# A decode step of attention and an MLP: TensorE's program in loops, a fixed home for V, and w4 loaded ahead of K

## The chip, the cores and the metric

The kernel runs on one core of a Trainium2 chip. The metric is the device time of one execution in microseconds (us); lower is better. The engines are called by the profile's names: PE (TensorE), DVE (VectorE), ACT (ScalarE), POOL (GpSimd) and SP (SyncE), which issues the large loads. PSUM is the memory that PE writes to, in eight banks of 128 x 512 float32 each.

## The reference

One token, x of 1024 values, passes a layernorm and then two branches whose results are added:

```
xn  = layernorm(x)
A:  q = xn @ wq                                     # 32 heads of 128
    scores = q . k_cache * 128**-0.5                # 4 key heads, 65536 keys each, 8 query heads share one
    o = softmax(scores) @ v_cache ;  A = o @ wo     # wo is 4096 x 1024
B:  h  = gelu(layernorm(xn) @ w1) ; hs = shift(h) @ w2      # with one position every shifted value is zero
    x1 = xn + hs ; B = x1 + gelu(layernorm(x1) @ w3) @ w4   # w3 1024 x 3584, w4 3584 x 1024
out = x + A + B
```

All inputs are bfloat16. The two caches hold 4 x 65536 x 128 values each, 67 MB apiece; the weights together are about 36 MB. Every byte is used once.

## The kernel before

**Homes.** Three slots of 64 KB per partition lie in the on-chip memory. A cache is cut into eight tiles of 32768 keys: tile 0 and 1 belong to the first key head, 2 and 3 to the second, and so on. A K or a V tile fills a slot, 8.4 MB. Work items go through the three slots in turn:

```
wq, K0, V0, w3, K1, V1, wa, K2, V2, K3, V3, K4, V4, K5, V5, K6, V6, K7, wb, V7, wo
```

Here wa is w1 with the first half of w4, and wb is the second half of w4 with w2. Item i+3 is loaded by SP when item i has been used, so SP's queue normally holds one or two loads that have not begun. Only wo differs: it takes the slot of K7 and is loaded in five pieces of 10, 10, 8, 3 and 1 rows (a row is 1024 columns of one chunk of wo).

**One K tile** (`compute_K`). DVE transposes the tile in four quarters (L449, viewed as float32, so pairs of bfloat16 values move together). PE multiplies: 64 products of 128 x 512 into four banks `sc` (L455), in a loop over the banks, started after two quarters and again after four; in the last tile after every quarter. DVE takes the maximum over `sc` (L462), two tiny PE transposes with three small DVE steps between them make a maximum per query head (L463 to L469), ACT takes the exponential (L471), and DVE transposes the result into `work` (L473).

**One V tile** (`compute_V`). PE forms 64 products from `work` and the V slot into the bank `oacc` (L503), four at a time in four column strips of the array. After the first tile of a head ACT copies `oacc` away (L509). After the second, `group_weights` and `group_end` put the two tiles together: weighted sums on DVE (L488, L491, L515), one PE product (L521), a division and a reduction on DVE (L523 to L529). This fills 32 rows of `oT`, the operand of wo. wo's products need all four heads in `oT`.

**The ends.** wq, w3 and w1 are multiplied with 32 columns at once in strips (`rows_product`, L321). w4, w2 and the first ten rows of wo run in `rows_loop` (L337): a loop on PE, two products of 512 columns for each row, one column of results, two rows to a pass (five for wo). The other 22 rows of wo run unrolled in `compute_wo`, as four products of 256 columns in four strips (L536). A copy on DVE (L560) and one store end the kernel.

**Order.** `Flow` records each operation's reads and writes, and emits a wait on the semaphore of the engine or load that it needs. All engines run the recorded order; nothing moves it afterwards.

Of the kernel before, what the change touches and what calls it, by code (L numbers as in the profile page):

```python
# [6 lines left out]

BF16 = mybir.dt.bfloat16
# [8 lines left out]
WO_PIECES = (10, 10, 8, 3, 1)  # L17
WO_UNROLL = 5
CGS = 2


class Flow:


    def __init__(self, nc, ctx):
        self.nc = nc
        self.ctx = ctx
        self.engines = {"T": nc.tensor, "V": nc.vector, "S": nc.scalar, "G": nc.gpsimd, "Q": nc.sync}
        self.sems = {}
        self.counts = {}  # L30
        self.seen = {e: {} for e in self.engines}
        self.writer = {}
        self.readers = {}

    def sem(self, name):
        if name not in self.sems:
            self.sems[name] = self.ctx.enter_context(self.nc.semaphore(f"s_{name}"))
            self.counts[name] = 0
        return self.sems[name]

    def _wait(self, eng, reads, writes):
# [7 lines left out]
        for key in reads:  # L49
            if key in self.writer:  # L50
                token = self.writer[key]
                if token[0] != "T" or eng != "T":
                    add(token)
        for key in writes:
            if key in self.writer:
                token = self.writer[key]
                if token[0] != "T" or eng != "T":
                    add(token)
            for token in self.readers.get(key, ()):
                if token[0] != eng:  # L60
                    add(token)
        for name, value in need.items():
            if self.seen[eng].get(name, 0) < value:
                self.engines[eng].wait_ge(self.sem(name), value)
                self.seen[eng][name] = value
# [8 lines left out]
    def op(self, eng, reads, writes, emit, times=1):  # L74

        self._wait(eng, reads, writes)
        sem = self.sem(eng)

        def signal(ins):
            ins.then_inc(sem, 1)  # L80

        emit(signal)
        self.counts[eng] += times
        self._note((eng, self.counts[eng]), reads, writes)
# [8 lines left out]
    def one(self, eng, reads, writes, call):  # L93
        self.op(eng, reads, writes, lambda signal: signal(call(self.engines[eng])))
# [3 lines left out]
def kernel(  # L98
# [28 lines left out]
    assert S == 1 and DH == P and REP == 8 and HQ == 32 and DC == 8 and NOUT == 1024  # L127
# [4 lines left out]
    FW = F // 8  # L132
    assert FW <= 512 and F % 8 == 0 and FW % 16 == 0 and FW // 16 == FC and OC == 32
    NQ = NOUT // 4
    NH = NOUT // 2
    FH = FC // 2
# [9 lines left out]
    slots = [tile_sb([P, KEYS], BF16, f"slot{i}") for i in range(SLOTS)]  # L146
    work = tile_sb([P, HF * 512], BF16, "work")
    ob = tile_sb([P, 512], F32, "ob")
    xpad = tile_sb([P, DC, 32], BF16, "xpad")
    QS = P + 24  # L150
    qst = [tile_sb([P, 4, QS], BF16, f"qst{i}") for i in range(2)]
    qsel = tile_sb([P, 4, HQ], BF16, "qsel")
    ident_bf = tile_sb([P, P], BF16, "ident_bf")
    ident_f = tile_sb([P, P], F32, "ident_f")
    og = tile_sb([P, P + 1], F32, "og")
    msk = tile_sb([P, 4, 32], F32, "msk")
    hstrip = tile_sb([P, 192], BF16, "hstrip")
    gsel = tile_sb([P, P], BF16, "gsel")
    sel32 = tile_sb([P, 32], F32, "sel32")
    sel8 = tile_sb([P, 8], F32, "sel8")  # L160
    sel8x = tile_sb([P, 32], F32, "sel8x")
    mask16 = tile_sb([P, 16], F32, "mask16")
    mask64 = tile_sb([P, 64], F32, "mask64")
# [3 lines left out]
    lnb = tile_sb([P, 8, DC], F32, "lnb")  # L167
    x_bf = tile_sb([P, DC], BF16, "x_bf")
    xn2b = tile_sb([P, DC], BF16, "xn2b")
    qT = tile_sb([P, HQ], BF16, "qT")  # L170
    hf_f = tile_sb([P, FC], F32, "hf_f")
    hT = tile_sb([P, FC], BF16, "hT")
    gT = tile_sb([P, DC], BF16, "gT")
    o5 = tile_sb([P, 32], F32, "o5")
    oT = tile_sb([P, OC], BF16, "oT")
    rep = msk[0:1].rearrange("p a b -> p (a b)")

    sc = ps.tile([P, HF, 512], F32, name="sc")
    oacc = ps.tile([P, 512], F32, name="oacc")
    pm = ps.tile([P, 512], F32, name="pm")  # L180
    psR = ps.tile([P, 2, 512], F32, name="psR")
    psB = sc[:, 0, :]
# [7 lines left out]
    assert sum(WO_PIECES) == OC  # L190
    wo_start = [sum(WO_PIECES[:i]) for i in range(len(WO_PIECES))]

    items = [("wq",), ("K", 0, 0), ("V", 0, 0), ("w3",)]
    for g in range(HKV):
        for r in range(NT):
            if (g, r) != (0, 0):
                items += [("K", g, r), ("V", g, r)]
            if (g, r) == (0, 1):
                items += [("wa",)]
    items.insert(len(items) - 1, ("wb",))  # L200
    items += [("wo",)]
# [4 lines left out]
    one, op = fl.one, fl.op  # L206

    slot_of = [i % SLOTS for i in range(len(items))]
    slot_of[-1] = slot_of[items.index(("K", HKV - 1, NT - 1))]

    def load(i):
        item, s = items[i], slot_of[i]
        t, kind = slots[s], items[i][0]
        if kind == "wq":
            loads = [(0, wq_v)]
        elif kind == "w3":
            loads = [(0, w3_v)]
        elif kind == "wa":
            loads = [(0, w1_v), (KEYS // 2, w4_v[:, 0:FH * NOUT])]
        elif kind == "wb":  # L220
            loads = [(0, w4_v[:, FH * NOUT:FC * NOUT]), (KEYS // 2, w2_v)]
        elif kind == "wo":
            loads = [(wo_start[q] * NOUT, wo_v[:, wo_start[q] * NOUT:(wo_start[q] + n) * NOUT])
                     for q, n in enumerate(WO_PIECES)]
        else:
            cache = A_k_cache if kind == "K" else A_v_cache
            _, g, r = item
            loads = [(0, cache[0, g, r * KEYS:(r + 1) * KEYS, :].rearrange("(p k) d -> p (k d)", p=P))]
        fl._wait("Q", [], [("slot", s), ("slot", s, 1)] + [("slot", s, q) for q in range(2, 5)] + [("kt", s, cg) for cg in range(4)])
        for n, (at, src) in enumerate(loads):  # L230
            key = ("slot", s) if n == 0 else ("slot", s, n)
            fl.dma("Q", f"slot{s}" if n == 0 else f"slot{s}_{n}", [], [key], t[:, at:at + src.shape[-1]], src)

    qrow = work[:, 0:1024].rearrange("p (b n) -> p b n", b=2)
    psel = work[:, 1024:1536].rearrange("p (b m) -> p b m", b=4)
    ones_f = og[:, 0:P]
    xr = work[:, 1536:2048]

    load(0)
    fl.dma("S", "x", [], ["x_bf"], x_bf[:], A_x[0, 0, :].rearrange("(p c) -> p c", c=DC))  # L240
    load(1)
    load(2)
    one("G", [], ["xr"], lambda e: e.memset(xr[0:33, :], 0.0))
    fl.dma("S", "x2", [], ["xr"], xr[0:33:32, :], A_x[0, 0, :].rearrange("(j n) -> j n", j=2))

    def ident(t, key):
        one("G", [], [key], lambda e: e.memset(t[:], 0.0))
        one("G", [key], [key], lambda e: e.affine_select(
            out=t[:], in_=t[:], compare_op=ALU.not_equal, fill=1.0, base=0, pattern=[[-1, P]],
            channel_multiplier=1))  # L250

    eps_t, negmean, rstd, ln_s1, ln_s2 = (sm[:, i:i + 1] for i in range(5))
    ident(ident_bf, "ident_bf")
    ident(ident_f, "ident_f")
    one("G", [], ["eps"], lambda e: e.memset(eps_t, LN_EPS))
    one("G", [], ["ones"], lambda e: e.memset(ones_f, 1.0))
    one("G", [], ["xpad"], lambda e: e.memset(xpad[:], 0.0))
    one("G", [], [("qst", 0)], lambda e: e.memset(qst[0][:], 0.0))
    one("G", [], [("qst", 1)], lambda e: e.memset(qst[1][:], 0.0))
    one("G", [], ["hstrip"], lambda e: e.memset(hstrip[:], 0.0))  # L260

    def v(reads, writes, call):
        one("V", reads, writes, call)

    v(["ident_f"], ["sel32"], lambda e: e.tensor_tensor(out=sel32[:], in0=ident_f[:, 0:32], in1=ident_f[:, 32:64], op=ALU.add))
    v(["ident_f", "sel32"], ["sel32"], lambda e: e.tensor_tensor(out=sel32[:], in0=sel32[:], in1=ident_f[:, 64:96], op=ALU.add))
    v(["ident_f", "sel32"], ["sel32"], lambda e: e.tensor_tensor(out=sel32[:], in0=sel32[:], in1=ident_f[:, 96:128], op=ALU.add))
    v(["sel32"], ["mask16"], lambda e: e.tensor_tensor(out=mask16[:], in0=sel32[:, 0:16], in1=sel32[:, 16:32], op=ALU.add))
    v(["ident_f"], ["mask64"], lambda e: e.tensor_tensor(out=mask64[:], in0=ident_f[:, 0:64], in1=ident_f[:, 64:128], op=ALU.add))
    v(["sel32"], ["dmask"], lambda e: e.reduce_sum(out=dmask[:], in_=sel32[:].rearrange("p (cg h) -> p cg h", h=8), axis=AX.X))  # L270
    v(["sel32"], ["mask4"], lambda e: e.reduce_sum(out=mask4[:], in_=sel32[:].rearrange("p (x dd) -> p dd x", dd=4), axis=AX.X))
    v(["sel32"], ["sel8"], lambda e: e.reduce_sum(out=sel8[:], in_=sel32[:].rearrange("p (cg h) -> p h cg", h=8), axis=AX.X))
    v(["sel8"], ["sel8x"], lambda e: e.tensor_copy(out=sel8x[:].rearrange("p (h dd) -> p h dd", dd=4),
                                                   in_=sel8[:].unsqueeze(2).to_broadcast([P, 8, 4])))
# [331 lines left out]
```

## Time and profile before

| what | value |
|---|---|
| median of 3 runs | 402.25 us (402.10 to 402.31) |
| profiled execution, its own time | 402.23 us |
| span of its profile | 400.1 us |
| moved by DMA | 170.02 MB, 425 GB/s over the span |
| DMA queue of SP (q1), share of 16 engines | 98.3% |
| busy: PE, DVE, ACT, POOL | 223.5, 210.5, 30.9, 6.3 us |
| mean granted TensorE clock | 0.80 |

The span runs from the first to the last instruction of the profiled execution; 2.1 us of its time lie outside. Busy times overlap, so no engine's share says by itself what it costs. A line such as L449 is a line of the kernel.

### The profile page before, as it was taken

Reading aid. Unit: us, or ns where it says so; the run is one execution under the profiler, and the core shown is the slowest. Engines: PE = TensorE matmul, PEld = TensorE weight load, DVE = VectorE, ACT = ScalarE, POOL = GpSimd, SP = SyncE. Lnnn points to the kernel's source line nnn. Section 1 sums busy time; section 2 is a strip of 40 time slices with the busy share of each in tenths; the row PEclk is TensorE's granted clock in tenths of the full one; section 3 lists DMA queues with packets and bytes.
Section 4 is the critical chain, followed back from the end, with each engine's and each line's share of the span. In section 5 each row is a group of like instructions: output and inputs, shape, how many; then the busy total and the mean of one; then the engine's idle time right before and its main releaser. Section 6 shows DMA issues by size and latency. Waiting matters only on the chain.

```text
span 400.1 us, 4118 instructions
## 1 busy us (share of the span) xinstructions
PE 223.5 (56%) x1407; PEld 91.3 (23%) x1407; DVE 210.5 (53%) x191; ACT 30.9 (8%) x36; POOL 6.3 (2%) x28
## 2 busy tenths in 40 slices
PE   0263087360195563964395608845925194596985
PEld 0220033130042220421142203312402041232332
DVE  2201792210962448822972499269455963794421
ACT  1000000320001300003001000020020002000200
POOL 3000000000000000000000000000000000000000
PEclk9995579585589598795699567968988599799799
DMA  8999999999989999999999999999999999999995
GB/s 347 465 446 419 420 414 454 391 473 452 426 382 471 451 426 414 426 432 432 465 434 426 419 426 439 426 472 428 426 419 434 439 419 459 398 454 434 397 432 208
DMA packets 4054, 170.02 MB, mean 425 GB/s; under 512 B 582, under 2 KB 588, under 8 KB 844
## 3 DMA queue, kind: packets, MB, share of 16 engines
q1 hardware_dynamic: 3896, 169.87, 98.3%
q8 instruction: 8, 0.13, 0.1%
q10 hardware_dynamic: 148, 0.00, 0.0%
q14 instruction: 2, 0.02, 0.0%
HBM read 169.87 MB, written 0.00 MB: 425 GB/s over the span
## 4 chain that ended last, share of the span: by engine, by line
DMA 53%; PE 28%; DVE 13%; issue 4%; ACT 1%; SPq 1%; POOL 0%; ACTq 0%
DMA slot<-in_A_k_cache_dram 46%; PE sc L455 20%; DVE slot L449 10%; DMA slot<-in_A_wo_dram 7%; PE oacc L503 5%; PE psR L337 2%; DVE sm L462 2%; DVE work L473 1%; ACT work L471 1%; SPq L89 1%; PE sc L321 0%; DVE og L515 0%; ACT L471 0%; DVE sm L464 0%; PE pm L463 0%
## 5 line engine op out<-in xcount | busy, mean ns | idle before, releaser
L455 PE MATMUL sc<-slot,qst 128*128 x512 | 127.8, 407 | 77.4 <-DVE slot L449 76.4
L449 DVE STREAM_TRANSPOSE slot<-slot 128x4096 f32<-128x4096 f32 x32 | 139.4, 4413 | 29.7 <-DMA slot<-in_A_k_cache_dram 29.7
L455 PEld LDWEIGHTS sc<-slot,qst 128*128 128x128 bf16 x512 | 51.8, 101 | 154.2 <-issue 106.8
L503 PE MATMUL oacc<-slot,work 128*32 128x512 bf16 x512 | 45.7, 530 | 37.5 <-DVE work L473 21.9
L462 DVE TENSOR_REDUCE sm<-sc 128x1 f32<-128x2048 f32 x8 | 18.3, 2291 | 58.4 <-PE sc L455 58.4
L503 PEld LDWEIGHTS oacc<-slot,work 128*32 128x32 bf16 x512 | 19.0, 127 | 60.8 <-issue 56.9
L473 DVE STREAM_TRANSPOSE work<-work 128x2048 bf16<-128x2048 bf16 x8 | 18.5, 2312 | 21.2 <-ACT work L471 21.2
L471 ACT ACTIVATE work<-sc,sm 128x2048 bf16<-128x2048 f32 x8 | 15.7, 1967 | 147.1 <-DVE sm L469 147.1
L337 PE MATMUL psR<-slot,hT 128*1 x56 | 16.2, 438 | 0.5 <-issue 0.2
L515 DVE SCALAR_TENSOR_TENSOR og<-oacc,sm,og 128x128 f32<-128x128 f32 x16 | 5.6, 351 | 18.6 <-PE oacc L503 18.2
L321 PE MATMUL sc<-slot,xpad 128*32 128x512 bf16 (+1 forms) x144 | 11.1, 441 | 4.3 <-DMA slot<-in_A_wq_dram 4.3
L471 ACT ACT_TABLE_LOAD x3 | 3.8, 1283 | 117.5 <-DVE sm L469 117.5
L463 PE MATMUL pm<-ident_f,sm 128*1 128x128 f32 x8 | 2.2, 270 | 19.1 <-DVE sm L462 19.1
L294 PE MATMUL pm<-sm,og 128*128 128x1 f32 x4 | 1.2, 363 | 14.9 <-DVE sm L293 14.9
L337 PEld LDWEIGHTS psR<-slot,hT 128*1 x56 | 5.1, 92 | 10.9 <-issue 7.8
L321 PEld LDWEIGHTS sc<-slot,xpad 128*32 128x32 bf16 x144 | 5.4, 113 | 9.0 <-DMA slot<-in_A_wq_dram 4.4
L399 DVE TENSOR_TENSOR work<-pm,mask 128x448 f32<-128x448 f32 x1 | 0.6, 624 | 11.0 <-PE pm L394 11.0
L463 PEld LDWEIGHTS pm<-ident_f,sm 128*1 128x1 f32 x8 | 0.6, 79 | 23.0 <-DVE sm L462 23.0
L352 DVE CAST work<-sc 128x512 bf16<-128x512 f32 x1 | 0.7, 690 | 9.2 <-PE sc L321 9.2
L347 POOL COPY qst<-qsel 32x32 bf16<-32x32 bf16 x12 | 2.5, 206 | 189.0 <-PE sc L455 161.8
L337 PE MATMUL psR<-slot,oT 128*1 x20 | 4.5, 379 | 1.6 <-DVE oT L529 1.6
L509 ACT COPY ob<-oacc 128x512 f32<-128x512 f32 x4 | 2.3, 585 | 33.1 <-PE oacc L503 33.1
(99 smaller groups left out, 71.6 us busy)
## 6 DMA issues: line engine op xcount, KB each, us to landing
slot<-in_B_w_dram SPq DMA_DIRECT2D x1, 7168.0 KB, 50.8
slot<-in_B_w_dram SPq DMA_DIRECT2D x2, 3584.0 KB, 31.9
slot<-in_A_wo_dram SPq DMA_DIRECT2D x2, 2560.0 KB, 19.5
slot<-in_B_w_dram SPq DMA_DIRECT2D x2, 2048.0 KB, 30.1
slot<-in_A_wo_dram SPq DMA_DIRECT2D x1, 2048.0 KB, 26.7
slot<-in_A_wo_dram SPq DMA_DIRECT2D x1, 768.0 KB, 28.1
slot<-in_A_wo_dram SPq DMA_DIRECT2D x1, 256.0 KB, 28.4
slot<-in_A_k_cache_dram SPq DMA_DIRECT2D x8, 36.1
```

What stands on the lines that cost most here:

```text
L89: self.engines[eng].dma_start(out=out, in_=in_).then_inc(sem, 16)
L321: ins = nc.tensor.matmul(sc[32 * j:32 * j + 32, bk, 0:width], lhsT=xpad[:, c, :], rhs=wt[:, c, ch * width:(ch + 1) * width], start=(c == 0 ...
L337: ins = nc.tensor.matmul(psR[0:1, h, :], lhsT=lv[:, bass.ds(c, 1), u], rhs=wv[:, bass.ds(c, 1), u, h, :], start=False, stop=False, skip_gr ...
L347: lambda e: e.tensor_copy(out=qst[g % 2][sl, :, 24 + 32 * a:24 + 32 * a + 8], in_=qsel[sl, :, 8 * g:8 * g + 8]))
L449: v([("slot", s)], [("kt", s, cg)], lambda e: e.transpose(out=kf[:, cg, :], in_=kf[:, cg, :]))
L455: ins = nc.tensor.matmul(sc[:, bass.ds(hf, 1), :], lhsT=qst[g % 2][:, bp, 24 - 8 * cg:24 - 8 * cg + P], rhs=kr[:, cg, bass.ds(hf, 1), :, b ...
L462: v(["sc"], ["mx"], lambda e: e.reduce_max(out=mx, in_=sc[:].rearrange("p h n -> p (h n)"), axis=AX.X))
L463: one("T", ["mx", "ident_f"], ["pm"], lambda e: e.transpose(pm[0:1, 0:P], mx, ident_f[:]))
L471: one("S", ["sc", ("nball", r)], WORK + [("lall", r)], lambda e: e.activation(out=pT, in_=sc[:], func=ACTF.Exp, bias=nball[:, r:r + 1], sc ...
L473: v(["work"], ["work"], lambda e: e.transpose(out=pT, in_=pT))
L503: ins = nc.tensor.matmul(oacc[32 * u:32 * (u + 1), :], lhsT=pT[:, hf, 32 * t:32 * (t + 1)], rhs=vt[:, :, hf, t, :], start=(hf == 0 and t < 4),
L515: v(["oacc", ("wm", 1), "og"], ["og"], lambda e: e.scalar_tensor_tensor(out=og[:, 0:P], in0=oacc[:, P * cg:P * (cg + 1)], scalar=wm[:, 1, ...
```

## The change

The kernel is rewritten in these parts; the numbers of products and the bytes loaded stay as they are, but for small ones.

1. **TensorE's program is written by itself** (`tensor_program`), as nested loops: over four heads, two tiles, four banks. It takes tokens from two semaphores, `VT` (given by DVE) and `GT` (given by POOL), waiting for one and then lowering it. The other engines run their recorded program; both are wrapped in a loop of one pass (`once`) with a branch hint for each engine.
2. **K's quarters are cut by bank, not by column group**: after each transposed quarter PE makes the sixteen products of one bank. The maximum is taken over three banks, then over the fourth.
3. **Homes are fixed**: V always lies in slot A, K by turns in C and B. V of tile t+1 is therefore loaded when the V product of tile t is over, and K of tile t+2 right after it in SP's queue.
4. **All weights but wo come first**: wq, w3, w4 (24 rows) with w2, w1 with w4 (4 rows), K0, V0, K1, V1, ... K7, V7, wo. K7 is loaded in halves, V7 as three quarters and one quarter.
5. **Products with x, w1 and w4 have one column of results**; the rows that they make are turned into columns by a DVE transpose and small products. The layernorms run on one partition, largely on ACT.
6. **The sums over a head's first tile move from DVE to POOL**, but for the last head.
7. **wo**: pieces of 12, 9, 3, 3, 4 and 1 rows. The first 27 rows run in a loop of three rows to a pass, each pass with a token from POOL; then DVE adds their sum to the residual (`fold`), and the last five rows run unrolled in strips.

```diff
-WO_PIECES = (10, 10, 8, 3, 1)
-WO_UNROLL = 5
-CGS = 2
+WO_PIECES = (12, 9, 3, 3, 4, 1)
+WO_LOOP = 27
+K_LAST = (2, 2)
+V_LAST = (3, 1)
+UNROLL = 4
+UNROLL_WO = 3
...
+    def take(name, n=1):
+        te.wait_ge(tokens[name], n)
+        te.sem_inc(tokens[name], -n)
...
+        def rows_pass(c, at, unroll, dst):
+            for u in range(unroll):
+                for h in range(2):
+                    ins = te.matmul(dst[0:1, h, :] if unroll == UNROLL_WO else dst(h), lhsT=cols[:, bass.ds(c + u, 1)],
+                                    rhs=home[:, bass.ds((c + u) * NOUT + at + h * NH, NH)],
+                                    start=False, stop=False, skip_group_check=True)
+            ins.then_inc(sig, 1)
...
+        with te.Fori(0, 2) as p:
+            with te.Fori(p * DC, p * (ROWS_A + ROWS_B - DC) + DC - UNROLL + 1, UNROLL) as c:
+                rows_pass(c, B * KEYS - ROWS_A * NOUT, UNROLL, lambda h: banks[0:1, bass.ds(p * 6 + h, 1), :])
...
+        with te.Fori(0, HKV):
+            with te.Fori(0, NT) as r:
+                with te.Fori(0, HF) as hf:
+                    take("VT")
+                    for cg in range(4):
+                        for bp in range(4):
+                            ins = te.matmul(sc[:, bass.ds(hf, 1), :], lhsT=qst[:, bp, 24 - 8 * cg:24 - 8 * cg + P],
+                                            rhs=kv[:, bass.ds(r * (2 * 4 * HF) + hf * 4 + cg, 1), :, bp // 2, :, bp % 2],
+                                            start=(cg == 0 and bp == 0), stop=(cg == 3 and bp == 3), skip_group_check=True)
+                    ins.then_inc(sig, 1)
+                take("VT")
+                te.transpose(pm[0:1, 0:P], sm[:, 50:51], ident_f[:]).then_inc(sig, 1)
+                take("VT")
+                te.transpose(pm[:, P:P + 1], rep[0:1, :], ident_f[0:1, 0:1]).then_inc(sig, 1)
+                for hf in range(HF):
+                    take("GT")
+                    for t in range(16):
+                        u, y = t % 4, 16 * hf + t
+                        ins = te.matmul(oacc[32 * u:32 * (u + 1), :], lhsT=work[:, 32 * y:32 * (y + 1)], rhs=vt[:, hf, :, t, :],
+                                        start=(y < 4), stop=(y >= 60), tile_position=(0, 32 * u))
+                ins.then_inc(sig, 1)
+            take("VT")
+            te.matmul(pm[0:32, 0:P + 1], lhsT=sel8x[:], rhs=og, start=True, stop=True).then_inc(sig, 1)
+
+        with te.Fori(0, WO_LOOP - UNROLL_WO + 1, UNROLL_WO) as c:
+            take("GT")
+            rows_pass(c + (2 * DC + FC), C * KEYS - (2 * DC + FC) * NOUT, UNROLL_WO, psR)
...
+        for hf in range(HF):
+            v([], [("kt", ks, hf)], lambda e: e.transpose(out=kf[:, hf, :], in_=kf[:, hf, :]), tok="VT",
+              peek=[("slot", ks, piece_of("K", t, hf)), "qst"], guard=[("sc", hf)])
...
+        v(SC[0:3], ["mx2"], lambda e: e.reduce_max(out=mx2[:, 0:1], in_=sc[:, 0:3, :].rearrange("p h n -> p (h n)"), axis=AX.X))
+        v(SC[3:4], ["mx2b"], lambda e: e.reduce_max(out=mx2[:, 1:2], in_=sc[:, 3, :], axis=AX.X))
...
+        for q, n in enumerate((HF,) if not last else V_LAST):
+            fl.token("G", ["work", ("slot", A, q)], "GT", n)
...
+            weights("V" if last else "G")
+        fl.pe(["work"] + [("slot", A, q) for q in range(4)], ["oacc"])
+        if not last:
+            load_tile("V", t + 1)
+            if t + 2 <= last_t:
+                load_tile("K", t + 2)
+            else:
+                load(C, wo_pieces)
...
+    for q, n in enumerate(WO_PIECES):
+        if wo_start[q] < WO_LOOP:
+            fl.token("G", ["oT", ("slot", C, q)], "GT", n // UNROLL_WO)
+            fl.pe(["oT", ("slot", C, q)], ["psR"], n // UNROLL_WO)
+    v(["psR", "work"], ["fold"], lambda e: e.tensor_tensor(out=fold, in0=psR[0:1].rearrange("o a n -> o (a n)"), in1=fold, op=ALU.add), tok="VT")
```

Built, TensorE's program has 143 rows (repeats of one line and shape counted as one row) where it had 434.

## The prediction

> **What bounds the kernel now.** I read the page's slices and queues first, then DVE's timeline for when K tiles land, then the end of PE's timeline.
>
> ```profile
> PEclk9995579585589598795699567968988599799799
> DMA  8999999999989999999999999999999999999995
> ...
> q1 hardware_dynamic: 3896, 169.87, 98.3%
> q8 instruction: 8, 0.13, 0.1%
> ```
>
> The DMA row is at nine from the first slice to the last but one. SP's queue fills 98.3% of 400.1 us, 393.3 us. The rest, 6.8 us, is all there is to win from loading, and it is the head and the end. So the kernel is bound by loading, and a change of order can only lose unless it shortens the last microseconds.
>
> ```profile
> 151.11 17.42 DVE L449 STREAM_TRANSPOSE slot<-slot 128x4096 f32<-128x4096 f32 x4 [2.84 <-DMA slot<-in_A_k_cache_dram]
> 189.91 17.42 DVE L449 STREAM_TRANSPOSE slot<-slot 128x4096 f32<-128x4096 f32 x4 [4.24 <-DMA slot<-in_A_k_cache_dram]
> 232.84 17.42 DVE L449 STREAM_TRANSPOSE slot<-slot 128x4096 f32<-128x4096 f32 x4
> 267.13 17.43 DVE L449 STREAM_TRANSPOSE slot<-slot 128x4096 f32<-128x4096 f32 x4 [0.89 <-DMA slot<-in_A_k_cache_dram]
> ```
>
> Rows released by DMA give the landing of a K tile. From K2 (151.11) to K3 (189.91) a V and a K tile passed: 38.8 us; K3 to K5 (267.13) took 77.2, so 38.6 a pair and 19.3 a tile. The row at 232.84 has no DMA behind it: DVE was late for that tile and loading did not care, because the three slots held more work.
>
> ```profile
> 147.37 6.40 PE L337 MATMUL psR<-slot,hT 128*1 x24 [0.17 <-issue]
> ...
> 223.10 6.51 PE L503 MATMUL oacc<-slot,work 128*32 128x512 bf16 x64 [4.78 <-issue]
> ...
> 300.35 5.45 PE L503 MATMUL oacc<-slot,work 128*32 128x512 bf16 x64 [4.78 <-issue]
> ...
> 387.52 4.04 PE L337 MATMUL psR<-slot,oT 128*1 x18 [1.62 <-DVE oT L529]
> ...
> 394.08 1.04 PE L536 MATMUL sc<-slot,oT 128*1 128x256 bf16 x32 [0.45 <-DMA slot<-in_A_wo_dram]
> 395.93 0.50 PE L536 MATMUL sc<-slot,oT 128*1 128x256 bf16 x12 [0.81 <-DMA slot<-in_A_wo_dram]
> 396.65 0.28 PE L536 MATMUL sc<-slot,oT 128*1 128x256 bf16 x4 [0.21 <-DMA slot<-in_A_wo_dram]
> ```
>
> The last rows are the end: `oT` is ready near 387.2, and from then PE waits for pieces of wo; the last lands at 396.6. Twenty-two rows of wo in strips are cheap: eight take 1.04 us, 0.13 each. A row in the loop is two products: 0.43 us at five rows to a pass (18 in 4.04), 0.53 at two to a pass (24 products in 6.40, 0.267 each).
>
> **The parts that loading hides.** The bytes are the same; three more pieces of loads add perhaps 0.2 us (estimate). The refills of instructions in q8 are 0.1% of 16 engines, 6.4 engine-us over eight packets: 0.8 us each on one engine. A load lands with its slowest engine, so all eight gone is worth 0 to 0.8 us; I take 0, since one left delays as much as eight on eight engines.
>
> *Head.* wq's 64 products of one column, at 0.22 to 0.27, take 14 to 17 us from about 24.5 (wq lands at 23.05 by L321; the layernorm on one partition is some twenty small steps of 0.15 to 1.3 us). w1 with w4 is issued near 41 and needed when SP's first three loads end, near 58. w3's 56 products end near 57, so K0 is issued 8 us before its turn. The 88 products of w1, w4 and w2 run from about 67 to 91; K0 lands near 87 (K1's 99.17 less 12 us of bytes that now come later) and needs PE from 91.5. If all this is 3 us later nothing starves. Cost 0.
>
> *Middle.* V's one home is the new wait: on SP, V of tile t+1 and behind it K of t+2 stand behind the V product of t. Count from a K landing: transposes 17.42; PE starts 0.35 later (52.0 busy to first product at L455) and the last bank's sixteen products take 3.65 at full clock: 21.45. Earlier, all 64 came after half the transposes, 24.95 (267.13 to 292.09); this is a gain of 3.5 us that loading does not use. Maximum of one bank about 0.8 (a quarter of L462's 2.29, a short one more); the two tiny transposes with their DVE steps 1.4, the exponential 2.1, the transpose of `work` 2.3; tokens, two on PE and one through POOL, 0.1 to 0.3 each by the gaps of other handoffs (0.02 to 0.35), say 0.5; V product 5.45 to 6.51, say 6.0. Sum 34.6. From SP's issue to first bytes: at least the issue itself, 0.4; at most 2.8, what wq's landing leaves (23.05 less 0.95 and 19.3); I take 1.5. So V is queued 36.1 after K landed, and the queue runs dry at 38.6: 2.5 us to spare (1.2 to 3.6). After a second tile of a head, `group_end` (3.2 us from 229.64 to 232.84) ends at 37.8, still ahead of the next landing. Cost 0 while the sum is under 38.6. The three sums moved to POOL run in V's 6 us; POOL's L347 and memset rows (0.2 to 0.6 us for 100 to 600 elements) put them at 1 to 4 us together; above 6 they would hold `group_end` back.
>
> **The end, where the cost is.** In place of wb, only V7 and wo follow K7. wo still ends at 396.8. Backwards at 19.3 a tile and small pieces: V7 lands at 377.3, K7's second half at 357.9, the first at 348.2.
> - Two quarters are left: 8.7 to 366.6; last bank +0.35 + 3.65 = 370.6.
> - Softmax and `work`: 0.8 + 1.4 + 2.1 + 2.3 + 0.5 = 7.1: 377.7, just behind V7.
> - V product 6.0: 383.7. `group_end` 3.0 (one cast less): `oT` at 386.7, against 387.2 before.
> - Token and start 0.4: 387.1. Now 27 rows, 54 products, in passes of three. Bounds: 0.213 each, where the sequencer keeps ahead as with five rows: 11.5. Above: the loop of two rows needs 1.07 per pass where its products need 0.86, so its sequencer is the limit; three rows have half as many steps more, extra register steps (the built program shows one for each row) and the token: 1.9 a pass, 17. I take 0.267 as in the loop nearest in size: 14.4, ending 401.5, drained at 401.7. [...] wo landed at 396.8 and no longer matters.
> - `fold` on DVE over 1024 elements: twice L548's 0.68, less its start, 1.2: 402.9. Its eight products on PE with the last row: 0.15 + 0.61 + 0.13 + 0.28 = 1.2: 404.1. In the old kernel the fold lay beside loading.
> - Copy 0.45, then 2.7 from the copy's end (397.4) to the end of the span: 407.2.
>
> Against 400.1 this is +7.1: 402.2 + 7.1 = 409.3 us. The profiled execution and the median differ by 0.02, so no correction.
>
> **A clock that may be low.** The V product's two lengths are the granted clock:
>
> ```profile
> 300.65:304.06 3.41, 3.41 (x36) 1.44 (x32) 1.69 (x8) 0.00 (x0) 0.00 (x0) 0.50 1.11 480
> 304.06:307.48 3.42, 1.80 (x33) 0.74 (x26) 1.40 (x4) 0.00 (x0) 0.00 (x0) 1.00 0.87 369
> 307.48:310.89 3.41, 0.34 (x2) 0.07 (x2) 2.89 (x5) 0.00 (x0) 0.00 (x0) 1.00 1.02 442
> ```
>
> The clock column (third from the end) rises after one busy window of 3.4 us, and stays up through a window with PE busy 1.80 and one of 0.34; only then it falls. PE is idle for 3.4 us before wo's loop, but for one small product. If a window of little work ends there, some 3.4 us of the loop run at half clock: 0.42 a product (12 of L455 in 5.01 from 108.31) against 0.267, which costs 1.3 us. I take no such loss, at 4 in 10 that it comes.
>
> **Rivals.**
> - *The middle starves.* If the chain from a K landing to V's issue exceeds 38.6, each of seven tiles pays the excess: 1 us over gives +7, 416. For: the margin is 2.5 and tokens, POOL and loop jumps are unmeasured. Against: all large terms are rows. Chance 0.12. [...]
> - *The head is late once*: layernorm and the rows on one partition 5 us slower than counted, 2 us of empty queue: 411.3. Chance 0.06.
> - *Faster.* wo's products keep up with loading and no refill is left: the end goes to 396.6 - 0.8 + 3.5 = 399.3, or 401.4 and a little less. This decides when 27 rows and the fold are over by 396, so `oT` would be needed before 382, ahead of V7's product. Against: V7 lands at 377.3. Chance 0.03.
> - *Nothing changes*: the loop ends as the last piece lands, 402.2. Needs nearly the same. Chance 0.03.
>
> **How the numbers follow.** Forecast 0.76, at 409.3. Its bounds: 11.5 for the loop is -2.9, a refill lag and a V product at full clock another -1.3, so 405; 17 for the loop +2.6 and the low clock +1.3, so 413.2. To hold 8 in 10, with the head's case and the low part of the starving case in it: 405.0 to 414.5. Of this kernel 0.2% (0.8 us) can be told from no change. Faster 0.03, same 0.03, slower 0.94.
>
> **What would show it.** DMA at nine up to V7 and wo, no idle DVE longer than the 4 us of before ahead of K tiles; `oT` near 387; 54 products of wo at 0.25 to 0.3 with no DMA among their releasers; the span's end 10 us after the last landing of wo instead of 3.5. I am wrong if gaps stand in the middle of the DMA row, or if wo's loop waits for landings.

## The result, and the profile after

The changed kernel takes 412.25 us (median of 6 runs, 411.68 to 413.40), the kernel before 402.28 us beside it (6 runs, 402.10 to 402.34). The ratio is 1.0254, with a 95% interval of 1.0237 to 1.0271: slower by 10 us. The profiled execution took 412.29 us with a span of 410.5 us; 1.8 us lie outside it, against 2.1 before.

From the page of the changed kernel: the slices of the DMA engines, SP's queue, and the groups of instructions of wo's loop and of the fold.

```profile
DMA  9999999999999999999999999999999999999960
...
q1 hardware_dynamic: 4328, 169.87, 96.3%
...
L305 PE MATMUL banks<-home,cols 128*1 x142 | 36.9, 404 | 7.0 <-PEq L271 5.8
L560 DVE TENSOR_TENSOR scratch<-banks,scratch 1x1024 f32<-1x1024 f32 x1 | 1.2, 1212 | 16.3 <-PE banks L305 16.3
```

There is no gap in the middle of the DMA row, but its end is new: a slice (10.3 us) at six and one at zero. SP's queue fills 96.3% of 410.5 us, 395.3 us: 2.0 more than before. So about 2 us of the loss could come from loading and the rest is an end in which nothing is loaded. The packets of instructions in q8, eight before, are gone.

K's landings, from DVE's timeline of the changed kernel (the first column is the start, which is the landing where DMA stands behind it):

```profile
124.44 17.42 DVE L518 STREAM_TRANSPOSE home<-home 128x4096 f32<-128x4096 f32 x4 [8.83 <-DMA home<-in_A_k_cache_dram]
...
163.98 17.42 DVE L518 STREAM_TRANSPOSE home<-home 128x4096 f32<-128x4096 f32 x4 [2.51 <-DMA home<-in_A_k_cache_dram]
...
202.58 17.43 DVE L518 STREAM_TRANSPOSE home<-home 128x4096 f32<-128x4096 f32 x4 [10.10 <-DMA home<-in_A_k_cache_dram]
...
242.04 17.42 DVE L518 STREAM_TRANSPOSE home<-home 128x4096 f32<-128x4096 f32 x4 [2.24 <-DMA home<-in_A_k_cache_dram]
```

The steps are 39.5, 38.6 and 39.5 us, and so on to K6 at 320.11; before, a pair took 38.6 to 38.8. Every second pair loses 0.9 us, of which more below.

The end, from the timeline of the changed kernel (start, duration, engine and line, idle time before with its releaser):

```profile
378.96 5.01 PE L339 MATMUL banks<-home,scratch 128*32 128x512 bf16 x64 [4.90 <-POOLq L90]
...
386.67 0.36 DVE L510 TENSOR_REDUCE cols<-scratch 32x32 bf16<-32x128 f32 x1
387.53 8.65 PE L305 MATMUL banks<-home,cols 128*1 x30 [1.47 <-PEq L271]
396.52 1.46 PE L305 MATMUL banks<-home,cols 128*1 x6 [0.34 <-PEq L271]
...
401.88 1.46 PE L305 MATMUL banks<-home,cols 128*1 x6 [0.32 <-PEq L271]
403.38 1.21 DVE L560 TENSOR_TENSOR scratch<-banks,scratch 1x1024 f32<-1x1024 f32 x1 [16.35 <-PE banks L305]
...
404.74 0.61 PE L353 MATMUL banks<-scratch,ident_f 1*1 1x256 f32 x8 [0.96 <-PEq L271]
...
405.27 0.28 PE L353 MATMUL banks<-home,cols 128*1 128x256 bf16 x4
405.61 0.42 DVE L563 CAST scratch<-banks 97x256 bf16<-97x256 f32 x1 [1.02 <-PE banks L353]
406.06 0.63 SPq L99 DMA_DIRECT2D out_dram<-scratch  x1
```

`oT` is ready at 387.03 us, before at about 387.2. From there all is serial and waits for no load. Nine passes of three rows run from 387.53 to 403.34, 15.8 us; a pass takes 1.79 us, of which six products take 1.46 and 0.33 goes by ahead of the next one, where PE's sequencer branches back and takes its token (L271). Then the fold, 1.21 us, and its products, and the copy ends at 406.03, against 397.40 before. That is +8.6 us. The other +1.8 us lies behind the copy: from its end to the end of the span 4.5 us pass, before 2.7. 8.6 + 1.8 is the 10.4 us between the two spans. Where the 1.8 us come from stands in SP's waits (waiting line, what it waited for, us in total, times, longest):

```profile
SPq L222 <- DVEq L222: 2.4, 1, 2.4
```

At the end all engines wait for a semaphore that SP sets, and SP then for each of them. In the trace's instruction records SP sets it at 406.94, ACT and PE pass at 406.98 and 406.99, and DVE, whose loop of one pass ended with a branch (L115) at 405.72, only at 409.43. In the trace's packet records a packet of instructions (8 KB) runs from 407.65 to 408.03, between that branch and that step.

### The profile page after: what moved, and what is told of

It reads as the page before. It is cut to its first block, busy times and chain, and to the rows that moved or that the text cites. A ratio compares the mean times of both kernels' runs of the same rounds, so it can differ in the third digit from the quotient of the medians.

```text
span 410.5 us, 4325 instructions
## 1 busy us (share of the span) xinstructions
PE 244.5 (60%) x1345; PEld 97.0 (24%) x1345; DVE 214.5 (52%) x159; ACT 37.7 (9%) x42; POOL 12.7 (3%) x41
## 3 DMA queue, kind: packets, MB, share of 16 engines
q1 hardware_dynamic: 4328, 169.87, 96.3%
## 5 line engine op out<-in xcount | busy, mean ns | idle before, releaser
L518 DVE STREAM_TRANSPOSE home<-home 128x4096 f32<-128x4096 f32 x32 | 139.5, 4414 | 55.9 <-DMA home<-in_A_k_cache_dram 55.9
L327 PE MATMUL banks<-home,qst 128*128 x512 | 127.0, 408 | 55.7 <-PEq L271 55.6
L327 PEld LDWEIGHTS banks<-home,qst 128*128 128x128 bf16 x512 | 51.9, 102 | 130.0 <-issue 80.1
L339 PE MATMUL banks<-home,scratch 128*32 128x512 bf16 x512 | 45.1, 529 | 40.5 <-PEq L271 35.6
L305 PE MATMUL banks<-home,cols 128*1 x142 | 36.9, 404 | 7.0 <-PEq L271 5.8
L532 ACT ACTIVATE scratch<-banks,sm 128x2048 bf16<-128x2048 f32 x8 | 15.7, 1967 | 204.2 <-DVE sm L531 204.1
L339 PEld LDWEIGHTS banks<-home,scratch 128*32 128x32 bf16 x512 | 19.1, 128 | 63.2 <-issue 59.6
L534 DVE STREAM_TRANSPOSE scratch<-scratch 128x2048 bf16<-128x2048 bf16 x8 | 18.5, 2311 | 18.7 <-ACT scratch L532 18.7
L280 PE MATMUL banks<-home,xn 128*1 x64 | 15.8, 413 | 12.6 <-PEq L271 12.6
L522 DVE TENSOR_REDUCE sm<-banks 128x1 f32<-128x1536 f32 x8 | 14.0, 1748 | 2.1 <-PE banks L327 2.0
L280 PE MATMUL banks<-home,cols 128*1 x56 | 12.2, 379 | 2.7 <-DVE scratch L446 2.7
```

The lines of the kernel that those rows point to most:

```text
L280: ins = te.matmul(banks[0:1, bass.ds(ch, 1), :], lhsT=lhsT[:, c:c + 1], rhs=slot(s)[:, bass.ds(ch * 512 + c * width, 512)], start=(c == 0) ...
L305: ins = te.matmul(dst[0:1, h, :] if unroll == UNROLL_WO else dst(h), lhsT=cols[:, bass.ds(c + u, 1)], rhs=home[:, bass.ds((c + u) * NOUT + ...
L327: ins = te.matmul(sc[:, bass.ds(hf, 1), :], lhsT=qst[:, bp, 24 - 8 * cg:24 - 8 * cg + P], rhs=kv[:, bass.ds(r * (2 * 4 * HF) + hf * 4 + cg ...
L339: ins = te.matmul(oacc[32 * u:32 * (u + 1), :], lhsT=work[:, 32 * y:32 * (y + 1)], rhs=vt[:, hf, :, t, :], start=(y < 4), stop=(y >= 60), ...
L518: v([], [("kt", ks, hf)], lambda e: e.transpose(out=kf[:, hf, :], in_=kf[:, hf, :]), tok="VT", peek=[("slot", ks, piece_of("K", t, hf)), " ...
L522: v(SC[0:3], ["mx2"], lambda e: e.reduce_max(out=mx2[:, 0:1], in_=sc[:, 0:3, :].rearrange("p h n -> p (h n)"), axis=AX.X))
```

## The experiments

The theory: the loss is serial work behind `oT` (wo's loop with its tokens, then the fold), and DVE's late end. A second one, which grew out of K's landings: loads of V are queued so late that loading slips, mostly unseen because the end is later still. The rivals: the half clock, the number of products in a pass, the order with all weights ahead of K7, or the rest of TensorE's looped program.

### e1_strips: 12 rows in the loop instead of 27

```diff
-WO_LOOP = 27
+WO_LOOP = 12
```

> The changed kernel with only the first 12 rows of wo in the loop; the other 20 run unrolled in strips and the fold comes after row 12. Theory A (the loss is the end: 27 rows of wo at 0.6 us each begin when oT is ready, then the fold in series): four passes from 387.5 end near 395, the fold lies beside loading, the strips end 0.5 us after wo's last landing at 398; the span falls by 7 us and the time from 412.3 to near 405. Theory B (the loss is loading made slower by V's one home): wo's landing bounds the end, so the time falls by at most 1 us.

Measured: 408.28 us (4 runs, 406.06 to 409.88), ratio to the kernel before 1.0131 (1.0099 to 1.0163). The loop is worth 4 us here, less than expected, because in this profiled execution (409.88) loading was late: `oT` came at 391.0 and wo's last piece at 401.7, where the changed kernel's came at 397.9. The shorter end uncovers loading. This run started the second theory.

### e2_nine: nine rows to a pass

```diff
-WO_PIECES = (12, 9, 3, 3, 4, 1)
-UNROLL_WO = 3
+WO_PIECES = (9, 9, 9, 4, 1)
+UNROLL_WO = 9
```

> The changed kernel with nine rows of wo to a pass (three passes, pieces of 9, 9, 9, 4 and 1). If a pass of three is bound by PE's sequencer (6 products take 1.46 us in 1.79), longer passes run at 0.216 a product at full clock: 54 products in 11.7 to 13.5 us instead of 15.8, time 409 to 410. If the products themselves are the limit, 412.3.

Measured: 413.36 us (410.99 to 416.47), ratio 1.0274 (1.0210 to 1.0337); no gain in time. The 54 products of the profiled execution took 14.7 us:

```profile
389.69 14.28 PE L305 MATMUL banks<-home,cols 128*1 x52 [1.47 <-PEq L271]
```

In its clock records half clock reigns to 395.6: some 14 products at 0.43 us there, then 40 at 0.216, 8.7 us. With long passes the sequencer is no limit, and the half clock costs about 3 us instead. `oT` was 2 us late in this execution as well, so what the loop won, loading lost.

### e3_nohint and e4_noloop: the loop of one pass around DVE, ACT, POOL and SP

Without the branch hint (both `once` loops), and without that loop at all:

```diff
# e3
-            nc.engines[e].br_lt(regs, 1, on_true=f"{name}_loop", on_false=f"{name}_end").branch_hint(mark)
+            nc.engines[e].br_lt(regs, 1, on_true=f"{name}_loop", on_false=f"{name}_end")
# e4
-    rest.enter_context(once(nc, OrderedEngineSet([E.DVE, E.Activation, E.Pool, E.SP]), "rest"))
```

> The changed kernel without the branch hints. Theory A1 (the last 1.7 us are DVE waiting for code after its loop's end because the hint had the loop's start fetched): DVE's last step comes at once, time 410.5. Rival A2 (the code behind the loop is not at hand with or without a hint): time 412.3, unchanged. Theory B: unchanged.

> The changed kernel with the recorded program of DVE, ACT, POOL and SP standing in no loop of one pass; TensorE's stays in one. A1 and A2 both: the store's landing is followed by the end in 1.0 us as before, time 410.5. Theory B (nothing at the end, the 1.7 us are the store itself): 412.3.

Measured: 412.20 us (410.40 to 415.31), ratio 1.0273 (1.0230 to 1.0315), and 411.83 us (410.17 to 414.24), ratio 1.0258 (1.0220 to 1.0295). The profiled executions are the fastest of each, 410.40 and 410.17; in both, 2.7 us pass from the copy's end to the end of the span, as before; in e3 DVE passes the last wait at 406.86, 0.01 us from ACT and PE, and not 2.4 us behind them. So the 1.8 us are there in the profile, but the other runs scatter by 4 to 5 us and hide them in the median. The profiled executions of all runs agree. In the five that have the hint (the changed kernel, e1, e2, e7 and e8) 4.3 to 5.5 us lie behind the copy, and a packet of instructions begins 1.6 to 1.9 us after DVE's branch. In e3, e4, e9, e10 and e12 it is 2.7 us, and no such packet runs behind the copy. So in the profiles the hinted loop is the cause, and a packet of instructions goes with it; for which engine it is, the records do not say. In the medians e10 points the same way, less clearly.

### e5_order and e11_order: the order alone, in the kernel before

e5 puts wb ahead of K7, so that only V7 and wo follow K7; wo keeps K7's slot. e11 also loads wo into wb's slot, as soon as wb's products are over, and makes w2's products with wb's.

```diff
# e5
-    items.insert(len(items) - 1, ("wb",))
+    items.insert(len(items) - 2, ("wb",))
# e11, besides
-    slot_of[-1] = slot_of[items.index(("K", HKV - 1, NT - 1))]
+    slot_of[-1] = slot_of[items.index(("wb",))]
-        if it == ("K", HKV - 1, NT - 1):
+        if it == ("wb",):
             load(len(items) - 1)
```

> The kernel before with wb (half of w4, and w2) loaded ahead of K7 instead of behind it, nothing else. Theory A (the new order costs nothing by itself while wo's rows in strips keep up with loading): oT stays near 387 and the time within 1 us of 402.3. Rival (less work between K7 and wo brings the chain of K7 and V7 behind the last landing): 404 or more.

> The kernel before with wb loaded and used ahead of K7 (its w2 products there too), and wo loaded into wb's slot as soon as wb's products are over, so that only V7 and wo follow K7, as in the changed kernel. Theory (the order alone costs nothing while 22 rows of wo run in strips behind the last pieces): oT near 387 to 388, wo lands at 396.6, 402.0 to 403.0. Rival (putting all weights ahead of K7 is itself what makes the end late): 405 or more, with oT after 392.

Measured: 412.27 us (411.29 to 413.45), ratio 1.0253 (1.0228 to 1.0277), and 412.70 us (410.13 to 414.60), ratio 1.0251 (1.0216 to 1.0285). In both the theory failed and the rival came true. After e5 I blamed wo's home: wo was issued at 379.89 only, and loading stood still for some 5 us. e11 refutes that: wo is issued at 358.6 and lands at 397.0, and the time is the same. The timeline of e11 shows why:

```profile
357.71 17.42 DVE L450 STREAM_TRANSPOSE slot<-slot 128x4096 f32<-128x4096 f32 x4 [15.09 <-DMA slot<-in_A_k_cache_dram]
...
387.83 6.33 PE L504 MATMUL oacc<-slot,work 128*32 128x512 bf16 x64 [4.78 <-issue]
...
397.76 6.90 PE L337 MATMUL psR<-slot,oT 128*1 x18 [1.58 <-DVE oT L528]
```

K7, loaded whole, lands at 357.7 instead of 344.4, and 30.1 us pass from there to V7's product (in e5 it starts at 388.07). So in the old program the order costs 10 us at `oT`: 397.4 against 387.2. The changed kernel makes the same move and still has `oT` at 387.0, because it loads K7 in halves and multiplies bank by bank: from the second half's landing (358.90) to V7's product (378.96) are 20.1 us. Of the 10 us between 30.1 and 20.1, 8.7 are the transposes of half a tile, 17.42 less 8.77. This is read from the rows: no run loads K7 whole in the changed kernel. My mistake in both expectations was to leave the whole K7 out.

### e6_loop27: the kernel before, with 27 rows in loops of three

```diff
-WO_PIECES = (10, 10, 8, 3, 1)
-WO_UNROLL = 5
+WO_PIECES = (12, 9, 3, 3, 4, 1)
+WO_UNROLL = 3
...
-            if q == 0:
+            if q <= 3:
...
```

> The kernel before with only its end changed: wo's pieces 12, 9, 3, 3, 4, 1 and the first 27 rows in loops of three rows to a pass, the fold after them. Theory A: the same loss in the old kernel, less the tokens and the fold's single step: nine passes of 1.35 to 1.5 us from 387.5 end near 400.5, time 407 to 408.5. Theory B: wo's rows still hide beside loading, 402.3 to 403.

Measured: 404.77 us (404.33 to 405.11), ratio 1.0059 (1.0042 to 1.0075): +2.5 us, less than expected. From its timeline:

```profile
386.36 11.78 PE L337 MATMUL psR<-slot,oT 128*1 x52 [1.62 <-DVE oT L529]
...
398.61 0.68 DVE L550 COPY work<-psR 1x512 f32<-1x512 f32 x1 [12.61 <-PE psR L337]
```

The same 54 products are over in 12.2 us, 1.36 a pass. So of the changed kernel's 1.79 us a pass, 0.43 us are not the three rows: 3.9 us in nine passes. Both loops signal once a pass; what the changed kernel's has besides is the token and other register steps. Which of these takes how much was not separated. The fold is shared by DVE and ACT here (0.68 us).

### e7_clock: TensorE kept busy ahead of wo's loop

Eleven small products around the last product of `group_end` are to hold the clock up:

```diff
+            for _ in range(5):
+                te.matmul(banks[0:1, 0, 0:128], lhsT=ident_f[:, 0:1], rhs=ident_f[:], start=True, stop=True, skip_group_check=True)
             take("VT")
             te.matmul(pm[0:32, 0:P + 1], lhsT=sel8x[:], rhs=og, start=True, stop=True).then_inc(sig, 1)
+            for _ in range(6):
+                te.matmul(banks[0:1, 0, 0:128], lhsT=ident_f[:, 0:1], rhs=ident_f[:], start=True, stop=True, skip_group_check=True)
```

> The changed kernel with eleven products into an unused bank around the last small product of each head, so that PE is not idle between V7 and wo's loop. If the half clock that the profile shows from 388.6 to 392.0 costs what the passes say (two passes take 0.4 to 0.8 us more than their pace), the time falls by 0.5 to 1.3; if the sequencer hides it, the time is 412.3 or a little more.

Measured: 413.64 us (412.85 to 415.27), ratio 1.0296 (1.0275 to 1.0318). First the windows of the changed kernel in question (granted clock third from the end), then the loop of e7 in its timeline:

```profile
385.25:388.60 3.35, 1.45 (x7) 0.61 (x8) 1.15 (x4) 0.02 (x1) 0.00 (x0) 1.00 0.98 407
388.60:392.00 3.40, 3.31 (x9) 0.93 (x8) 0.00 (x0) 0.00 (x0) 0.00 (x0) 0.50 0.98 412
```

```profile
387.86 1.46 PE L305 MATMUL banks<-home,cols 128*1 x6 [0.17 <-issue]
389.71 1.46 PE L305 MATMUL banks<-home,cols 128*1 x6 [0.40 <-PEq L271]
...
402.28 1.45 PE L305 MATMUL banks<-home,cols 128*1 x6 [0.34 <-PEq L271]
```

With the six products of every pass at 1.45 to 1.46 us, as at full clock in the changed kernel, the loop takes 15.9 us, the same as with 3.4 us of half clock in it (15.8). The half clock is hidden: in the changed kernel's records products then run without a gap, 0.43 us each, and catch up later in the 0.33 us that the sequencer leaves in each pass. So for the changed kernel's profiled execution that rival is refuted; e12 below shows a loop too short to catch up.

### e8_vpieces: V in halves

Each V tile but the last is loaded in two halves, the first issued when the V product has used its part; PE signals after every bank instead of after the fourth.

```diff
+V_CUT = (2, 2)
...
-                ins.then_inc(sig, 1)
+                    ins.then_inc(sig, 1)
```

> The changed kernel with every V tile but the last loaded in two halves, the first as soon as half of the V product before it is done, some 3 us earlier. If the 39.5 us between every other pair of K landings (38.6 between the rest) come from V's one home being refilled too late, all pairs take 38.6 to 38.8, wo lands 1 us earlier and the time falls by 1 to 1.5. If they come from something else in loading, the time stays or grows by 0.6 for the seven more pieces.

Measured: 411.26 us (409.86 to 411.91), ratio 1.0214 (1.0190 to 1.0237). K lands at 125.02, 163.78, 202.49, 241.18, 279.81 and 318.50 us: 38.7 a pair, all alike, and wo's last piece at 396.1 instead of 397.9. The time gains 1.0 us only, since the end does not wait for wo: `oT` comes 0.9 us earlier, at 386.09.

### e9_best, e10_vp_noloop, e12_whole_v: the terms put together

e9 has V in halves (e8), no loop of one pass (e4) and 9 rows of wo in the loop. e10 is e9 with the 27 rows in the loop; e12 is e9 with V loaded whole.

```diff
-WO_PIECES = (12, 9, 3, 3, 4, 1)
-WO_LOOP = 27
+WO_PIECES = (9, 9, 8, 5, 1)
+WO_LOOP = 9
```

> The changed kernel with V loaded in halves (as in e8_vpieces), the loop of one pass around the program of DVE, ACT, POOL and SP left out (as in e4_noloop), and only 9 rows of wo in the loop, the other 23 in strips (pieces of 9, 9, 8, 5 and 1 rows). Theory (the loss is wo's loop and the fold behind oT, plus DVE waiting for code at the end, plus loads queued too late): wo's last landing 396.1 as in e8, products over by 396.5, the end 2.7 to 3.5 us behind: 400.8 to 402.5, so within 0.3 per cent of the kernel before, perhaps 0.5 us below it. Rival (something in the rest of the new program, such as TensorE's own loops or the fixed homes, costs time of its own): 404 to 408, with wo landing after 398 or products still running then.

> As e9_best, but with the 27 rows of wo in the loop of three rows as in the changed kernel. Theory: loop and fold end near 405 whatever loading does, the tail behind the copy is 2.7 instead of 4.5: 409.0 to 409.8, which is 8 us above e9_best and 1.5 to 2 below e8_vpieces (411.3). Rival (DVE's late end is only a profile's matter, hidden in other executions): 411 to 411.5.

> e9_best with V loaded whole again, as in the changed kernel: only wo's loop is shortened to 9 rows and the loop of one pass is left out. Theory (a load of V that is issued 2 to 4 us before the queue is empty lands 0.9 to 2 us late, some or all of seven times): wo's last landing 398 to 402, time 403.5 to 406.5 with runs more than 2 us apart, so 1 to 4 us above e9_best (402.5). Rival (V's one home costs nothing once the end is short): 402.0 to 402.9, wo landing at 396.5.

| kernel | rows in the loop | one-pass loop | V | median, us (runs, from, to) | ratio to before (95%) |
|---|---|---|---|---|---|
| changed | 27 | yes | whole | 412.25 (6, 411.68 to 413.40) | 1.0254 (1.0237 to 1.0271) |
| e8 | 27 | yes | halves | 411.26 (4, 409.86 to 411.91) | 1.0214 (1.0190 to 1.0237) |
| e10 | 27 | no | halves | 409.51 (5, 409.07 to 411.11) | 1.0193 (1.0178 to 1.0208) |
| e9 | 9 | no | halves | 402.54 (12, 401.58 to 404.22) | 1.0015 (1.0003 to 1.0027) |
| e12 | 9 | no | whole | 406.37 (6, 404.45 to 407.88) | 1.0102 (1.0076 to 1.0127) |

e10 and e12 lie in the ranges of their theories, e9 0.04 us above the top of its own. From top to bottom the changed kernel loses 1.0 us by V's late loads, 1.75 us by the loop of one pass and 7.0 us by wo's loop. The 7.0 us are far outside the noise. The 1.75 us are not: the intervals of e8 and e10 overlap, and their ratios are 0.8 us apart. For that term the profiles above are the evidence. Without the three the changed kernel stands 0.03 to 0.27% above the kernel before, so for all else in the new program at most 1.1 us are left. The timeline of e9 shows an end that waits for loading again, as the old kernel's did:

```profile
386.63 1.46 PE L319 MATMUL banks<-home,cols 128*1 x6 [1.47 <-PEq L285]
...
391.77 1.21 DVE L575 TENSOR_TENSOR scratch<-banks,scratch 1x1024 f32<-1x1024 f32 x1 [5.64 <-PE banks L319]
...
395.93 0.89 PE L367 MATMUL banks<-home,cols 128*1 128x256 bf16 x24 [1.21 <-DMA home<-in_A_wo_dram]
396.87 0.42 DVE L578 CAST scratch<-banks 97x256 bf16<-97x256 f32 x1 [3.88 <-PE banks L367]
397.32 0.65 SPq L100 DMA_DIRECT2D out_dram<-scratch  x1
```

The fold now lies beside the landing of wo's last pieces, and the copy ends 397.29.

e12 shows what V's one home costs once the end is mended: 3.8 us instead of 1.0. SP's issues of V in e12, from its timeline:

```profile
122.31 0.33 SPq L99 DMA_DIRECT2D home<-in_A_v_cache_dram  x1
...
159.95 0.33 SPq L99 DMA_DIRECT2D home<-in_A_v_cache_dram  x1
...
200.09 0.33 SPq L99 DMA_DIRECT2D home<-in_A_v_cache_dram  x1
...
238.22 0.33 SPq L99 DMA_DIRECT2D home<-in_A_v_cache_dram  x1
```

and 278.50 and 316.58. The K tile queued ahead landed at 126.00, 165.35, 204.05, 243.66, 282.26 and 322.17, so the leads are by turns 3.7 to 4.0 and 5.4 to 5.6 us. The V tiles issued with the short lead landed 19.9, 20.2 and 20.5 us after that K, those with the long one 19.4, 19.3 and 19.3. A short lead costs 0.6 to 1.2 us each time here, although the load before was still running. It would also explain why the leads alternate: a late V puts the next K back, and that gives the V behind it a longer lead. wo's last piece lands at 400.1, 3.6 us later than in e9, and 2.8 us of that are these three. From that landing to the copy 1.35 us pass, in e9 0.38: `oT` came later too, at 390.3, and the loop met half clock from 389.9 to 396.7:

```profile
390.83 6.51 PE L305 MATMUL banks<-home,cols 128*1 x16 [1.47 <-PEq L271]
```

Fourteen of its 18 products ran at 0.43 us. The loop took 6.9 us, in e9 5.1: in three passes there is nothing left to catch up with, and the fold was over only then. So about 1 us of e12's excess comes from there.

The traces' records of landings say how far the short lead is the cause. They cover V1 to V6 in the seven traces that load V whole (the changed kernel, e1 to e4, e7 and e12). Of 24 loads with a lead of 3.2 to 4.4 us, 17 landed late, 0.3 to 1.6 us over the usual 19.3; the other seven, four of them in e3, were on time. Of 18 with 4.5 us and more, none took over 19.5. So a short lead makes a late landing likely, not certain. Why it costs was not traced further, nor why e9's own runs still spread over 2.6 us where the kernel before spreads over 0.6.

## Why the prediction was right

The forecast was 409.3 us in a range of 405.0 to 414.5; 412.25 lies inside, by the mechanism that was forecast: `oT` no earlier than before, then 27 rows and a fold in series behind it. By its own steps:

- **`oT` at 386.7:** 387.03. Every term of the chain held within 1 us, but two of them cancel by luck: K7's second half landed 1.0 us late (358.90 for 357.9), and the V product took 5.01 us, 2.83 of them at a granted clock of 0.50 and 2.18 at 1.00, instead of 6.0. e11 shows how much hung on the halves and the cut by bank, 10 us, which the sum had by its own count of K7's quarters.
- **wo's loop, 14.4:** 15.8, inside the bounds of 11.5 and 17, mis-sized by 1.4. I took the price of a product from the two-row loop, which the old kernel's trace shows at 0.216 as well (its last 14 products, from 375.8 on, run without a pause). So 0.267 was the price of one stretch and not of the loop, and the changed kernel's pass has a cost of its own. The 0.213 of the lower bound stands in no row: the products of the five-row loop follow each other at 0.215 to 0.216 (387.52 to 391.62 in the old kernel's trace). Of wo's loops here e2's long passes reach 0.216 us a product, e6's passes without tokens take 0.23 and the changed kernel's 0.30.
- **Fold and its products, 1.2 + 1.2:** from the last product's end (403.34) to the last row's (405.55) 2.2. Right. In the old kernel and in e9 it lies beside loading.
- **The end behind the copy, 2.7:** 4.5. This term failed: I carried it over from the old kernel, though the change put a loop's end there. The profiles of e3, e4 and e10 show the 1.8 us gone with the hint or with the loop. A packet of instructions stands in each of the five waits that have the hint; that DVE waited for that packet was not shown.
- **Middle, cost 0 with 2.5 to spare:** V was queued 34.1 to 35.3 us after K's landing, about as counted (34.6), while the load ahead had 3.3 to 5.4 us to go. The step that failed is the 1.5 us from issue to first bytes, which should have left some 2 us or more to spare: with up to 4.4 us to go a load mostly came late (17 of 24), with 4.5 and more it did not (0 of 18); why stays open. It cost 1.0 us of the changed kernel's median (e8). The rival of starving for longer, 1 us and more at each of seven tiles, did not come.
- **Refills of instructions, 0 to 0.8, taken at 0:** too low. In e1, e3, e7, e9 and e12 one packet of instructions (16 KB, 0.9 us) runs between 121.3 and 121.9, and K1 lands 20.4 to 20.8 us after V0; in the changed kernel, e2, e4, e8 and e10, without it, 19.3 to 19.8. The old kernel shows the same once, at V0 (20.6, a packet at 56.2); with its later packets a load of 8.4 MB took 19.3 to 19.5. In its records of landings each load has sixteen completions, and use waits for the last: K1's stands at 99.15, its transposes start at 99.17. V0's stand between 61.02 and 62.09 but for the last, at 62.94, 0.85 behind; after all eight packets those of wo's last piece stand in two groups, 394.66 to 395.18 and 396.11 to 396.60, 0.93 apart. So eight cost about what one did. The changed kernel thus won about 1.3 us here and lost more by V's late loads: wo's last piece landed at 397.9, counted at 396.8, before 396.6. The 0.2 us in that count for three more pieces was an estimate of mine that no run tests alone; in the old kernel wo's last two pieces, 768 and 256 KB, landed 1.85 and 0.71 us after the piece ahead, where their bytes at 19.3 us for 8.4 MB make 1.81 and 0.60.
- **Half clock, +1.3 at 4 in 10:** it came, 0.50 granted from 388.6 to 392.0, and cost nothing in 27 rows (15.8 us, in e7 15.9).
- **Head, cost 0:** w1 and w4 were issued at 42.4, K0 landed at 85.8, the rows of w4 and w2 ended at 91.7 and K0's products began at 92.6. V0 and K1 followed at 19.3 us each, so nothing starved. Right.

So the sum was 2.95 us short: 0.4 for the loop's later start (387.53 for 387.1), 1.4 for the loop and 1.8 for DVE's end, less 0.4 between the loop and the last row and 0.3 outside the span.

## What to carry to other kernels

In a kernel bound by loading, count the work left once the last operand is there, and keep it in the cheapest form: here a row in strips took 0.14 us (nine in 1.25, e9), one in a loop with a token to each pass 0.59 (27 in 15.8, the changed kernel). Queue the next load well before the queue runs dry, for instance by cutting the load in two: here 17 of 24 loads issued 3.2 to 4.4 us ahead landed late, none of 18 issued 4.5 us ahead and more, and halves of V won 1.0 us (e8). And a term that is hidden behind a later one (V's loads, 1.0 us) shows its whole price (3.8) only when that is gone.

## What the hardware showed that I had not expected

- After the branch at the end of a hinted loop of one pass DVE was 2.4 us late (1.1 to 2.6 in five traces) for a semaphore that ACT and PE passed at once, although their loops had the same end; without the hint it was not late (0.01 us from them in e3).
- Half clock for 3.4 us cost nothing in a loop whose sequencer left 0.33 us in each pass (15.8 us in the changed kernel against 15.9 in e7). A longer stretch of it cost about 3 us in three passes of nine rows (e2) and 1.8 us in three passes of three (e12).
- Of 24 loads of 8.4 MB issued 3.2 to 4.4 us ahead of the end of the one before, 17 landed 0.3 to 1.6 us late; of 18 issued 4.5 us ahead and more, none did.
- Beside one 16 KB packet of instructions, which took 0.9 us, a load of 8.4 MB landed 1.1 to 1.5 us late (K1 in five traces).
